# Gates of the second chunk scanned by themselves at the start of an mLSTM and Fourier-mix kernel

## The chip, the cores and the metric

The kernel runs on one core of one Trainium2 chip. The metric is the device time of one execution, in microseconds (us), as the median of several runs. Trace times are microseconds from the start of the profiled span. The engines are named as in the profile: PE is the matmul engine and PEld its weight loads, DVE the vector engine, ACT the engine of activations, POOL the general-purpose engine, and SP the one that issues the transfers.

## The reference, cut to what matters

The first block is an mLSTM cell over 4 batches of 8 heads, 768 tokens and a head dimension of 40; the second a Fourier mix with a two-layer MLP over the joined 320 features. All data are float32.

```python
for t in range(S):                                   # mLSTM, for every batch and head
    m_new = np.maximum(f_gate[t] + m, i_gate[t])     # running maximum
    f_stab, i_stab = np.exp(f_gate[t] + m - m_new), np.exp(i_gate[t] - m_new)
    m = m_new
    C = f_stab * C + i_stab * outer(v[t], k[t])
    n = f_stab * n + i_stab * k[t]
    y[t] = sigmoid(o_gate[t]) * (C @ q[t]) / np.maximum(np.abs(n @ q[t]), 1.0)
# x: y with the heads joined to 320 features
u = x + np.real(fft(fft(x, axis=1), axis=2))
out = u + relu(layernorm(u) @ w_ch1) @ w_ch2
```

## The kernel before, in words

**Chunks.** The 768 tokens are cut into 6 chunks (0 to 5) of 128. Within a chunk the recurrence becomes matrix products: scores of queries and keys (`mlstm_scores`, L458), times a matrix of exponentials W (`mlstm_exp`, L416, made on ACT; `mlstm_weigh`, L467, multiplies on DVE), times the values (`mlstm_from_chunk`, L482, PE). The state C carries what came earlier: `mlstm_from_state` (L473) reads it, `mlstm_to_state` (L489) makes a chunk's share on PE (the tile pc), and `mlstm_gather` (L503) brings on ACT the new state (L511) and the chunk's result (L524) out of PSUM and takes a tanh of the output gate (L529).

**Gates.** All this needs per-token numbers of the gates, which `gates` (L140) makes for all 4 batches and 8 heads at once: 32 partitions, one for each batch and head. `sums` (L190) is a running sum F of the forget gates within each chunk, a DVE scan. `maxima` (L194) subtracts F from the input gates (giving a), runs a second DVE scan for the running maximum M, and keeps nM and m_in, which are biases of later exponentials. `weights` (L238) makes `wk = exp(a + nM)` and `decay` (L242) makes `g = exp(m_in - M)`, one ACT instruction for each chunk. `columns` (L246) transposes a (j = 0) or wk (j = 1) on PE into a PSUM tile pt, so that tokens lie on partitions; a DVE copy brings that into colT. `spread_max` (L206) copies the maxima of four heads over all 128 partitions: a mask product in bf16 and then, for each head, a product of a one-hot column with M. That product is in float32 for the chunks 0 and 1. For the chunks 2 to 5 it is in bf16, with M cut by `parts` (L221), five POOL instructions, into three bf16 parts M3 whose sum is M. `spread_decay` (L230) does the like for g, into the tile pG.

Before the change chunk 0 goes through the gates alone, and the chunks 1 to 5 go through them together.

**Order.** The order of instructions on every engine is that in which the program issues them. After the lines written out in `gates`, calls are entered with `at(slot, phase, ...)` and issued by rising (slot, phase), where the phases EVAC, FILL, MAIN, FILL_PE are 0, 1, 2, 3. Chunk c of batch 0 begins at slot 3c. So in slot 4 ACT gets the gather of chunk 0 (FILL) and then the conversion of a block of MLP weights (FILL + 0.5, L351 and L352), and in slot 6 the exponentials of chunk 2. PE gets `decays` in slot 4 (tile pd), `spread_max` and `spread_decay` of chunk 2 at the end of slot 5, and in slot 6 `mlstm_from_state` and `mlstm_from_chunk` of chunk 1 and the scores of chunk 2.

**Buffers.** pt, the chunk results ph and the state shares pc take turns in two PSUM buffers (`ps_h`); the scores ps have two others (`ps_s`), which `mlstm_weigh` sets free.

Of the kernel before, what the change touches and what calls it, by code (L numbers as in the profile page):

```python
# [19 lines left out]
L = 128  # L20
NT = S // L
NP = H // 2
D1 = D + 1
BH = B * H
# [26 lines left out]
def kernel(  # L51
# [14 lines left out]
    nc = tc.nc  # L66
# [18 lines left out]
    def bank(name, shape, n=None):  # L85

        return ps_m.tile(shape, FP, name=name, tag=f"pm{next(turn) if n is None else n}")


    ident = const.tile([L, L], FP, name="ident")  # L90
# [6 lines left out]
    colT = const.tile([L, NT, 2, BH], FP, name="colT")  # L97
# [24 lines left out]
    def at(slot, phase, fn, *args):  # L122
        plan.setdefault((slot, phase), []).append((fn, args))
# [7 lines left out]
    EVAC, FILL, MAIN, FILL_PE = range(4)  # L131
# [8 lines left out]
    def gates(gp):  # L140
# [8 lines left out]
        M = gp.tile([L, NT, L], FP, name="M")  # L149
        wk = gp.tile([BH, NT, L], FP, name="wk")  # L150
        g = gp.tile([L, NT, L], FP, name="g")
        nM = gp.tile([BH, NT], FP, name="nM")
        M3 = gp.tile([3 * BH, NT, L], BF, name="M3")
        below = gp.tile([BH, NT, L], BF, name="below")
        sel = gp.tile([3 * BH, BH], BF, name="sel")
# [13 lines left out]
        nc.vector.memset(keep, 1.0)  # L169
        nc.vector.memset(keep[:, :, 0:1], 0.0)  # L170
        nc.vector.memset(shift, 0.0)
        nc.vector.memset(M[:, 0:2], 0.0)
        for t in C_bufs:
            nc.scalar.copy(out=t.rearrange("p (two n) t -> p two (n t)", two=2),
                           in_=rest.unsqueeze(1).to_broadcast([L, 2, 2 * L]))
# [11 lines left out]
        def flat(t, s):  # L187
            return t[0:BH, s].rearrange("p c t -> p (c t)")

        def sums(s):  # L190
            nc.vector.tensor_tensor_scan(out=flat(F, s), data0=flat(keep, s), data1=flat(f_sb, s), initial=0.0,
                                         op0=OP.mult, op1=OP.add)

        def maxima(s, initial):  # L194
            c0, c1 = s.start, s.stop
            nc.vector.tensor_tensor(out=a[:, s], in0=a[:, s], in1=F[:, s], op=OP.subtract)
            if c0 > 0:
                nc.vector.tensor_copy(out=shift[:, s, 0:1], in_=F[:, c0 - 1:c1 - 1, L - 1:L])
            nc.vector.tensor_tensor_scan(out=flat(M, s), data0=flat(shift, s), data1=flat(a, s), initial=initial,
                                         op0=OP.add, op1=OP.max)  # L200
            nc.vector.tensor_scalar(out=nM[:, s], in0=M[0:BH, s, L - 1], scalar1=-1.0, scalar2=None, op0=OP.mult)
            if c0 > 0:
                nc.vector.tensor_tensor(out=m_in[:, s], in0=M[0:BH, c0 - 1:c1 - 1, L - 1:L],
                                        in1=F[:, c0 - 1:c1 - 1, L - 1:L], op=OP.add)

        def spread_max(b, c, h0):  # L206

            k = chunks[b, c]
            if h0 == 0:
                k.W = wp.tile([L, H, L], FP, name="W", tag="W")  # L210
                k.M = []
            k.M.append(bank("pM", [L, NP, L]))
            nc.tensor.matmul(k.M[-1], ident_b, later_b.unsqueeze(1).to_broadcast([L, NP, L]), start=True, stop=False,
                             skip_group_check=True)
            for h in range(h0, h0 + NP):
                bh = b * H + h
                w, x = (ident[:, bh:bh + 1], M[:, c, :]) if c < 2 else (sel[:, bh:bh + 1], M3[:, c, :])
                nc.tensor.matmul(k.M[-1][:, h - h0, :], w.to_broadcast([w.shape[0], L]), x, start=False, stop=True,
                                 skip_group_check=True)

        def parts(s):  # L221

            m, rest_ = M[0:BH, s], shift[:, s]
            nc.gpsimd.tensor_copy(out=M3[0:BH, s], in_=m)
            nc.gpsimd.tensor_tensor(out=rest_, in0=m, in1=M3[0:BH, s], op=OP.subtract)
            nc.gpsimd.tensor_copy(out=below[:, s], in_=rest_)
            nc.gpsimd.tensor_copy(out=M3[BH:2 * BH, s], in_=rest_)
            nc.gpsimd.tensor_tensor(out=M3[2 * BH:, s], in0=rest_, in1=below[:, s], op=OP.subtract)

        def spread_decay(b, c):  # L230
            k = chunks[b, c]
            k.G = bank("pG", [L, NP, L])
            for h in range(H):
                r, bh = slice(h % 2 * 64, (h % 2 + 1) * 64), b * H + h
                nc.tensor.matmul(k.G[r, h // 2, :], ident[:, bh:bh + 1].to_broadcast([L, 64]), g[:, c, :],
                                 start=True, stop=True)

        def weights(s):  # L238
            for c in range(s.start, s.stop):
                nc.scalar.activation(out=wk[:, c], in_=a[:, c], func=AF.Exp, bias=nM[:, c:c + 1])  # L240

        def decay(s):  # L242
            for c in range(s.start, s.stop):
                nc.scalar.activation(out=g[0:BH, c], in_=M[0:BH, c], func=AF.Exp, scale=-1.0, bias=m_in[:, c])

        def columns(s, j):  # L246
            pt = ps_h.tile([L, NT, BH], FP, name="pt", tag="ph")
            for c in range(s.start, s.stop):
                nc.tensor.transpose(pt[:, c, :], (a, wk)[j][:, c, :], ident[0:BH, 0:BH])
            return pt  # L250

        first, others, last = slice(0, 1), slice(1, NT), slice(2, NT)
        sums(first)
        maxima(first, M_INIT)
        pt = columns(first, 0)
        nc.scalar.copy(out=colT[:, first, 0], in_=pt[:, first])
        weights(first)
        spread_max(0, 0, 0)
        pt = columns(first, 1)
        spread_max(0, 0, NP)  # L260
        mlstm_scores(0, 0)
        sums(others)
        mlstm_exp(0, 0, 0)
        nc.vector.tensor_copy(out=colT[:, first, 1], in_=pt[:, first])
        mlstm_exp(0, 0, NP)
        maxima(others, M[0:BH, 0, L - 1:L])
        pt = columns(others, 0)
        mlstm_load_o(0, 1)
        nc.vector.memset(g[:, 1:3], 0.0)
        nc.vector.tensor_copy(out=colT[:, others, 0], in_=pt[:, others])  # L270
        decay(slice(1, 2))
        weights(others)
        spread_max(0, 1, 0)
        spread_max(0, 1, NP)
        spread_decay(0, 1)
        pt = columns(others, 1)
        late = {"pt": pt}

        def clear(*tiles):
            for t in tiles:  # L280
                nc.gpsimd.memset(t, 0.0)

        def columns_late():
            nc.vector.tensor_copy(out=colT[:, others, 1], in_=late["pt"][:, others])

        def decay_late():
            decay(last)
            for hip in range(2):
                nc.sync.dma_start(out=G_d[1:NT, hip].rearrange("c p t -> p c t"), in_=g[hip:BH:2, 1:NT])

# [13 lines left out]
            nc.sync.dma_start(out=M_d.rearrange("c p t -> p c t"), in_=M[0:BH])  # L304

        at(12, FILL + 0.7, maxima_out)
        at(1, FILL + 0.2, parts, last)
        at(5, FILL_PE + 2.1, spread_decay, 0, 2)
        for c in range(2, NT):
            for h0 in (0, NP):  # L310
                at(3 * c - 1, FILL_PE + 2, spread_max, 0, c, h0)
        at(2, FILL + 0.5, columns_late)
        at(4, FILL - 0.4, decay_late)
        at(4, FILL + 0.5, decays)
        at(5, FILL - 0.5, decays_out)
# [95 lines left out]
    def mlstm_load_o(b, c):  # L411
        k = chunks[b, c]
        k.so = op_.tile([L, DM], FP, name="so", tag="so")
        nc.sync.dma_start(out=k.so, in_=o_gate[b, c])

    def mlstm_exp(b, c, h0):  # L416

        k = chunks[b, c]
        for h in range(h0, h0 + NP):
            M = k.M[h // NP][:, h % NP, :] if hasattr(k, "M") else k.W[:, h, :]  # L420
            nc.scalar.activation(out=k.W[:, h, :], in_=M, func=AF.Exp, scale=-1.0,  # L421
                                 bias=colT[:, c, 0, b * H + h:b * H + h + 1])
# [35 lines left out]
    def mlstm_scores(b, c):  # L458

        k = chunks[b, c]  # L460
        k.ps = [ps_s.tile([L, NP, L], FP, name=f"ps{hip}", tag="ps") for hip in range(2)]
        for p in range(NP):
            for hip in range(2):
                r = slice(hip * 64, hip * 64 + D)
                nc.tensor.matmul(k.ps[hip][:, p, :], k.qk[r, 1, p, :], k.qk[r, 0, p, :], start=True, stop=True)  # L465
# [599 lines left out]
    ctx.enter_context(tc.manual_schedule())  # L1065
    gates_pool = ExitStack()
    gates(gates_pool.enter_context(tc.tile_pool(name="gates", bufs=1)))


# [162 lines left out]
```

## Time and profile before

| | before |
|---|---|
| median of 3 runs (lowest to highest) | 422.28 us (421.28 to 422.81) |
| span of the profiled execution | 419.2 us |
| PE busy | 408.1 us, 97% |
| DVE busy | 288.8 us, 69% |
| ACT busy | 189.5 us, 45% |
| POOL busy | 112.9 us, 27% |
| PE busy between 4 and 20 us | 15.43 of 16 us |
| ACT busy between 12 and 20 us | 7.71 of 8 us |

The busy shares are means over a span with different stages; the change lies in the first 25 us. There PE and ACT are both nearly full, and DVE and POOL are busy for about three quarters and half of the time. The timeline lists the instructions of each engine in order, neighbours of one kind merged: start, duration, engine, line, operation, result and inputs, shapes and count.

### The profile page before, as it was taken

What the parts mean: (1) busy time and instruction counts of PE and PEld (TensorE: products, weight loads), DVE (VectorE), ACT (ScalarE), POOL (GpSimd) and SP (SyncE); (2) the same over time, 40 slices, a digit from 0 to 9 for tenths busy, and PEclk for the clock granted to TensorE, in tenths of its full rate; (3) what the DMA queues carried; (4) which work ended last, traced back from release to release, by engine and by line L of the source; (5) the groups of instructions that cost most, each with busy time, mean ns of one, the idle gap of its engine ahead of it and who ended that gap; (6) DMA issues with size and microseconds to landing.
All of it is one profiled execution on the core that took longest, in us unless ns stands there. A gap on an engine that the chain in (4) does not pass through costs nothing.

```text
span 419.2 us, 8001 instructions
## 1 busy us (share of the span) xinstructions
PE 408.1 (97%) x2966; PEld 302.4 (72%) x2966; DVE 288.8 (69%) x682; ACT 189.5 (45%) x493; POOL 112.9 (27%) x194
## 2 busy tenths in 40 slices
PE   8999999999999999999999999999999999999997
PEld 6877555566567778776549998976559988455996
DVE  8789895777895638777765569788663786335652
ACT  6986376686561222654455413744451113355000
POOL 5554201468431520442231430351220000020000
PEclk9999999999999999999999999999999999999999
DMA  7899297567765254276100554310000000000010
GB/s 230 288 250 318 71 278 257 185 162 219 236 189 164 59 155 139 64 210 197 50 0 2 156 149 131 100 42 1 0 2 0 33 31 34 0 2 0 16 48 31
DMA packets 20549, 47.14 MB, mean 112 GB/s; under 512 B 2784, under 2 KB 9312, under 8 KB 20384
## 3 DMA queue, kind: packets, MB, share of 16 engines
q1 hardware_dynamic: 20512, 46.65, 36.7%
q8 instruction: 23, 0.38, 0.4%
q14 instruction: 14, 0.11, 0.1%
HBM read 42.52 MB, written 4.11 MB: 111 GB/s over the span
## 4 chain that ended last, share of the span: by engine, by line
PE 82%; DVE 7%; DMA 4%; issue 3%; ACT 2%; POOL 1%; ACTq 0%; DVEq 0%; POOLq 0%; SPq 0%
PE po L999 18%; PE pm L897 17%; PE po L943 8%; PE pm L902 5%; PE ps L465 5%; PE ph L486 4%; PE pu L729 4%; PE ph L479 3%; PE pm L837 3%; DMA raw<-in_w 3%; PE px L535 2%; PE put L772 2%; PE pz L698 2%; DMA kvt<-in_kv 1%; PE pz L686 1%
## 5 line engine op out<-in xcount | busy, mean ns | idle before, releaser
L949 DVE SCALAR_TENSOR_TENSOR x<-po,rstd,x 128x160 f32<-128x160 f32 (+1 forms) x69 | 27.0, 395 | 40.2 <-PE po L999 34.1
L906 DVE TENSOR_TENSOR h<-h,pm 128x384 f32<-128x384 f32 x60 | 30.5, 550 | 30.5 <-ACT h L919 20.9
L421 ACT ACTIVATE W<-W,colT 128x128 f32<-128x128 f32 x144 | 45.0, 395 | 0.0
L443 POOL TENSOR_SCALAR_AFFINE_SELECT W<-W 128x1024 f32<-128x1024 f32 x18 | 21.6, 1198 | 81.0 <-ACT W L421 59.1
L943 PE MATMUL po<-w_sb,h 128*128 128x320 f32 x120 | 34.4, 435 | 0.0
L897 PE MATMUL pm<-uT,w_sb 128*128 128x384 f32 x90 | 32.8, 492 | 0.2 <-DVE uT L885 0.2
L471 DVE TENSOR_TENSOR W<-ps,W 128x512 f32<-128x512 f32 x48 | 30.7, 680 | 2.6 <-POOL W L443 2.4
L837 PE MATMUL pm<-uT,w_sb 128*128 128x384 f32 x80 | 29.6, 499 | 0.7 <-DVE x L749 0.5
L777 ACT COPY uT<-put 128x384 f32<-128x384 f32 x24 | 11.2, 478 | 40.2 <-PE put L772 40.2
L943 PEld LDWEIGHTS po<-w_sb,h 128*128 128x128 f32 x120 | 22.2, 190 | 9.5 <-issue 0.8
L999 PE MATMUL po<-T,S 128*128 128x160 f32 x180 | 27.9, 302 | 0.6 <-DVE x L949 0.6
L465 PE MATMUL ps<-qk 40*128 40x128 f32 x384 | 27.8, 284 | 0.0
L999 PEld LDWEIGHTS po<-T,S 128*128 128x128 f32 x180 | 25.5, 190 | 2.2 <-DVE x L949 1.0
L792 POOL TENSOR_TENSOR t<-rstd 128x6 f32<-128x6 f32 x12 | 2.9, 244 | 89.2 <-DVE v L790 88.6
L999 PE MATMUL po<-w_sb,h 128*128 128x160 f32 x180 | 26.4, 301 | 0.0
L465 PEld LDWEIGHTS ps<-qk 40*128 40x128 f32 x384 | 23.4, 187 | 4.1 <-issue 0.7
L999 PEld LDWEIGHTS po<-w_sb,h 128*128 128x128 f32 x180 | 25.1, 190 | 1.3 <-DVE x L949 0.3
L486 PE MATMUL ph<-W,kvt 128*41 128x128 f32 x384 | 25.8, 277 | 0.0
L431 POOL TENSOR_TENSOR qg<-qk,Gb 128x512 f32<-128x512 f32 x18 | 25.2, 1402 | 0.1
L524 ACT COPY h<-ph 41x512 f32<-41x512 f32 (+1 forms) x16 | 9.3, 583 | 34.9 <-PE ph L486 34.8
L479 PEld LDWEIGHTS ph<-qg,C 128*128 128x128 f32 x160 | 20.0, 191 | 6.3 <-issue 2.5
L897 PEld LDWEIGHTS pm<-uT,w_sb 128*128 128x128 f32 x90 | 16.2, 190 | 10.8 <-DVE h L906 1.5
(207 smaller groups left out, 864.6 us busy)
## 6 DMA issues: line engine op xcount, KB each, us to landing
W<-M_d SPq DMA_DIRECT2D x18, 512.0 KB
kvt<-in_kv SPq DMA_DIRECT2D x24, 324.0 KB
qk<-in_qkT SPq DMA_DIRECT2D x48, 160.0 KB
raw<-in_w SPq DMA_DIRECT2D x10, 640.0 KB
Gb<-G_d SPq DMA_DIRECT2D x36, 128.0 KB
so<-in_o SPq DMA_DIRECT2D x24, 160.0 KB
out<-x SPq DMA_DIRECT2D x24, 160.0 KB
ds_sb<-in_dft_s SPq DMA_DIRECT2D x1, 1155.0 KB
```

The lines of the kernel that those rows point to most:

```text
L421: nc.scalar.activation(out=k.W[:, h, :], in_=M, func=AF.Exp, scale=-1.0, bias=colT[:, c, 0, b * H + h:b * H + h + 1])
L431: nc.gpsimd.tensor_tensor(out=k.qg, in0=k.qk[:, 0], in1=k.Gb, op=OP.mult)
L465: nc.tensor.matmul(k.ps[hip][:, p, :], k.qk[r, 1, p, :], k.qk[r, 0, p, :], start=True, stop=True)
L471: nc.vector.tensor_tensor(out=Wv, in0=k.ps[hip], in1=Wv, op=OP.mult)
L479: nc.tensor.matmul(k.ph[:, p, :], k.C[:, p, :], k.qg[:, p, :], start=(p == 0), stop=False, skip_group_check=True)
L486: nc.tensor.matmul(k.ph[hip * 64:hip * 64 + D1, p, :], k.v1[:, 2 * p + hip, :], k.W[:, 2 * p + hip, :], start=(c == 0 and p == 0), stop=Tr ...
L837: nc.tensor.matmul(k.pm[i], w1_sb[:, ch, f0:f0 + L], u[2 * ch], start=(ch == 0), stop=False)
L897: nc.tensor.matmul(bank, w, u, start=start, stop=True, skip_group_check=True)
L906: nc.vector.tensor_tensor(out=h, in0=h, in1=bank, op=OP.add)
L943: nc.tensor.matmul(k.po, hidden(gr, f)[:, i * L:(i + 1) * L], w2_sb[:, f, :], start=(f == 0), stop=(f == NFF - 1))
L949: nc.vector.scalar_tensor_tensor(out=u, in0=po, scalar=k.rstd[:, c:c + 1], in1=u, op0=OP.mult, op1=OP.add)
L999: nc.tensor.matmul(po, a[:, f], w[:, f], start=start and f == 0, stop=f == half - 1, skip_group_check=True)
```

## The change

The gates of chunk 1 now go through the scans by themselves, directly after those of chunk 0, and those of the chunks 2 to 5 after them. Chunk 1's maxima are also cut into three bf16 parts, so that its `spread_max` uses the bf16 form. The purpose is to have what chunk 1 needs earlier, and to keep the other chunks' exponentials (`weights(others)`) from standing in front of those of chunk 1 on ACT: they go into the plan at slot 5, with their transpositions (`columns_last`) late in slot 5 and the copy into colT early in slot 6.

```diff
-        nc.vector.memset(M[:, 0:2], 0.0)
+        nc.vector.memset(M[:, 0:1], 0.0)
...
-                w, x = (ident[:, bh:bh + 1], M[:, c, :]) if c < 2 else (sel[:, bh:bh + 1], M3[:, c, :])
+                w, x = (ident[:, bh:bh + 1], M[:, c, :]) if c == 0 else (sel[:, bh:bh + 1], M3[:, c, :])
...
-        first, others, last = slice(0, 1), slice(1, NT), slice(2, NT)
+        first, second, others = slice(0, 1), slice(1, 2), slice(2, NT)
+        def columns_out(s, j, pt):
+            nc.vector.tensor_copy(out=colT[:, s, j], in_=pt[:, s])
...
         spread_max(0, 0, 0)
         pt = columns(first, 1)
+        sums(second)
+        maxima(second, M[0:BH, 0, L - 1:L])
+        parts(second)
+        columns_out(first, 1, pt)
+        pt = columns(second, 0)
         spread_max(0, 0, NP)
         mlstm_scores(0, 0)
+        mlstm_exp(0, 0, 0)
+        mlstm_exp(0, 0, NP)
+        mlstm_load_o(0, 1)
+        columns_out(second, 0, pt)
+        nc.vector.memset(g[:, 1:3], 0.0)
         sums(others)
-        mlstm_exp(0, 0, 0)
-        nc.vector.tensor_copy(out=colT[:, first, 1], in_=pt[:, first])
-        mlstm_exp(0, 0, NP)
-        maxima(others, M[0:BH, 0, L - 1:L])
-        pt = columns(others, 0)
-        mlstm_load_o(0, 1)
-        nc.vector.memset(g[:, 1:3], 0.0)
-        nc.vector.tensor_copy(out=colT[:, others, 0], in_=pt[:, others])
-        decay(slice(1, 2))
-        weights(others)
+        maxima(others, M[0:BH, 1, L - 1:L])
+        decay(second)
+        weights(second)
         spread_max(0, 1, 0)
         spread_max(0, 1, NP)
         spread_decay(0, 1)
-        pt = columns(others, 1)
-        late = {"pt": pt}
+        late = {1: columns(second, 1), 0: columns(others, 0)}
...
         def columns_late():
-            nc.vector.tensor_copy(out=colT[:, others, 1], in_=late["pt"][:, others])
+            columns_out(second, 1, late[1])
+            columns_out(others, 0, late[0])
+        def columns_last():
+            late[2] = columns(others, 1)
         def decay_late():
-            decay(last)
+            decay(others)
...
-        at(1, FILL + 0.2, parts, last)
+        at(1, FILL + 0.2, parts, others)
+        at(5, FILL + 0.3, weights, others)
+        at(5, FILL_PE + 1.8, columns_last)
+        at(6, FILL - 0.2, lambda: columns_out(others, 1, late[2]))
         at(5, FILL_PE + 2.1, spread_decay, 0, 2)
```

## The prediction

> **What bounds the kernel now.** I read the page first: busy shares, then the chain that ended last.
>
> ```profile
> PE 408.1 (97%) x2966; PEld 302.4 (72%) x2966; DVE 288.8 (69%) x682; ACT 189.5 (45%) x493; POOL 112.9 (27%) x194
> PE 82%; DVE 7%; DMA 4%; issue 3%; ACT 2%; POOL 1%; ACTq 0%; DVEq 0%; POOLq 0%; SPq 0%
> ```
>
> PE is busy for 97% of the span and carries 82% of the chain. So the end follows PE's queue: what delays PE early delays the end, unless a later idle stretch takes it up. After 24 us the gaps between PE's matmuls that are over 0.12 us add up to about 6 us, in pieces of at most 0.82 us.
>
> Next the chain in order of time, in the stage that the change touches.
>
> ```profile
> 16.14 0.44 PE pd L297 x2
> 16.58 0.32 PE pM L213
> 16.90 0.23 PE pM L218 x4
> 17.13 0.22 PE pM L213
> 17.35 0.23 PE pM L218 x4
> 17.57 1.02 PE pG L235 x16
> 18.60 1.09 PE ph L479 x8
> 19.68 1.09 PE ps L465 x16
> 20.78 1.00 PE ph L486 x16
> ```
>
> Columns are start, duration, engine, tile, line, count. The reader is to see that from pd on PE runs straight through: maxima and decay of chunk 2, then chunk 1's read of the state, chunk 2's scores, chunk 1's product with its values. Nothing here waits for ACT.
>
> (The chain also holds a transfer of kvt, 5.96 us from 36.87. I don't take it as a bound: no compute engine in the list of waits up to 50 us waits for a transfer, and PE works through most of that stretch.)
>
> Last the timeline of ACT from 10 to 20 us, with PE's and DVE's rows that matter.
>
> ```profile
> 10.62 1.26 DVE L471 TENSOR_TENSOR W<-ps,W 128x512 f32<-128x512 f32 x2
> 10.85 1.55 ACT L240 ACTIVATE wk<-a,nM 32x128 f32<-32x128 f32 x5
> 12.31 2.09 ACT L421 ACTIVATE W<-pM,colT 128x128 f32<-128x128 f32 x8
> 13.25 1.16 PE L465 MATMUL ps<-qk 40*128 40x128 f32 x16
> 14.31 1.26 ACT L244 ACTIVATE g<-M,m_in 32x128 f32<-32x128 f32 x4
> 15.24 0.48 PE L496 MATMUL pc<-vw,kvt 128*40 128x41 f32 x16
> 15.77 0.60 ACT L511 COPY C<-pc 40x164 f32<-40x164 f32 x2 [0.19 <-PE pc L496]
> 16.39 1.17 ACT L524 COPY h<-ph 41x512 f32<-41x512 f32 x2
> 16.51 0.39 PE L213 MATMUL pM<-later_b,ident_b 128*128 128x512 bf16 x1
> 17.59 0.47 ACT L529 ACTIVATE so<-so 128x320 f32<-128x320 f32 x1
> 17.96 0.82 ACT L351 ACTIVATE e<-e,ebias 128x640 uint32<-128x640 uint32 x1
> 18.68 0.72 ACT L352 ACTIVATE m<-m 128x640 f32<-128x640 uint32 x1
> 19.43 2.18 ACT L421 ACTIVATE W<-pM,colT 128x128 f32<-128x128 f32 x8
> ```
>
> ACT is full. From the end of pc (15.24 + 0.48 = 15.72) it needs until 19.43 for the gather of chunk 0 and the weight conversion. PE in that time is already at chunk 2's spread (16.51) and beyond.
>
> **What the Trainium skill says.** "TensorE: Matmul & The Clock Gate", section on the array's architectural detail, has ACT and DVE as strict FIFO, and PE as able to pull only weight loads ahead. The trace agrees: each engine's rows stand in program order. The same page, under what actually happens in the clock gate, halves PE's clock after an idle window of about 3.4 us and frees it after about as long a busy one. The trace fits its warm-up half: eight float32 matmuls of L218 take 1.48 us from 4.75 and 1.05 us from 6.57. "SBUF — State Buffer", who interferes with whom, has an exclusive lock between POOL and DVE instructions that use DVE's second port. The trace agrees: a DVE copy of 5 elements a partition (L198) takes 0.69 us and ends at 7.98, as POOL's vw ends at 7.95.
>
> **The change part by part.**
>
> *Bf16 spread for chunk 1.* In the chain the float32 form is 0.89 us for eight matmuls, and the bf16 form 0.23 us for four. Two halves save 2 x (0.89 - 0.23) = 1.32 us of PE. The M3 parts cost POOL five instructions on 128 elements instead of 512. At 512 the rows are 0.60 and 1.15 us; a quarter of the length lies between a quarter and all of that, and I take about 0.3 each with gaps, 1.7 us, from 5.6 (after chunk 1's scan) to 7.3. PE needs M3 only after the scores of chunk 0 at about 8.8, so that work hides it. The wait of 0.45 us for DVE's scan, ahead of the weights of L218 at 9.61, goes.
>
> *Fewer transpositions early.* PE has 6 instead of 10 ahead of chunk 1's scores (after chunk 0's own), about 0.06 us each: 0.24 us saved.
>
> So PE could begin chunk 1's scores early. Chunk 0's scores end at 8.8; two bf16 halves take 0.45 each (9.7); pG 1.02 (10.7), with its g from ACT at about 9.2, since ACT's exponentials of chunk 0 end at 8.81; five transpositions 0.3: 11.0, against 13.25.
>
> *The second scan on DVE.* It takes much of that back. Chunk 1's gates fit into the idle time from 4.4 to 6.45. Then come two colT copies and the memset of g (to 7.2), and the scans of 4 chunks: 0.35 us is the F scan of 128 elements and 1.47 that of 640, 2.19 ns an element, so 1.19 us for 512; likewise 1.25 for M (0.41 and 1.54). Subtraction 0.65, shift copy 0.1, nM and m_in 0.6. Sum: 7.2 + 1.19 + 0.65 + 0.1 + 1.25 + 0.6 = about 11.0. Only then does chunk 0's weighing (L471, 1.26 us) follow, ending at 12.3, or 13.0 if POOL's vw (0.73 us where nothing disturbs it) gets in front. It frees the two score buffers, so chunk 1's scores start at 12.35 to 13.05 instead of 13.25. From their start to the end of pc it is 15.72 - 13.25 = 2.47 us: pc ends at 14.8 to 15.5. Kept gain: 0.2 to 0.9 us.
>
> *The other chunks' exponentials.* Taking four of them out of the front lets ACT finish chunk 1's exponentials at about 11.8 and g at 13.1. But there ACT has to wait for pc, so this is worth nothing beyond the shift above.
>
> *The new wait.* This decides. `weights(others)` stands in slot 5, on ACT behind slot 4's gather and weight conversion. `columns_last` transposes its results on PE ahead of chunk 2's `spread_max`. Queued behind it on PE are that, pG, chunk 1's `mlstm_from_state`, chunk 2's scores and chunk 1's `mlstm_from_chunk`: all the rows of the second fence after pd. From the end of pc ACT needs 0.05 to start, 3.66 us to the end of the conversion (15.77 to 19.43), then four wk, 0.29 apart and the last 0.39 long: 0.87 + 0.39 = 1.26. The last wk is there 4.97 us after pc, the last transposition and the first mask product about 0.1 later: 5.1. Before, the mask product began 16.51 - 15.72 = 0.79 after pc. So PE loses 5.1 - 0.79 = 4.3 us; only pd (0.44) lies in its wait. ACT's exponentials of chunk 2, DVE's colT copy, and behind that on DVE qg and the join of the weights wait with it.
>
> *Sum.* 4.3 - 0.9 = +3.4 to 4.3 - 0.2 = +4.1 us at chunk 2's spread; middle 3.7. From there every wait is of the same kind as before, so I carry it to the end: 422.28 + 3.7 = 426.0. Transfers don't take it up: their engines rest from 45 to 50 us, and SP issues when buffers come free, which moves along. The memset of M and the moved loads cost nothing beside this.
>
> **The rivals.**
>
> *A: as above*, 425 to 427, 426.0.
>
> *B: the wait also drops PE's clock.* PE would rest from about 16 to 20 us, 3.6 to 4.4 us. Against the skill's window of 3.4 us, whose position isn't tied to the kernel, that may just suffice. Then some 3.4 us or more at half speed cost about 2.5 more: 428.5. For it: the slow matmuls at the start. Against it: no rest that long in the trace after the start, so nothing here shows the drop, and a whole window must fall into the rest.
>
> *C: the early gain is kept.* If DVE's order costs less than I think, PE keeps all of the 2.25 us (13.25 - 11.0), and the loss is 4.3 - 2.25 = 2.05: 424.3; with some slack later about 423.8. For it: DVE's numbers are chained from short rows. Against it: the score buffers hang on one DVE row that has four chunks' scans in front of it.
>
> *D: faster.* If the transpositions in fact don't hold PE (wk done in time by an ACT that has run ahead), what remains is the saving of 1.32 + 0.24 and perhaps the wait of 0.15 between matmuls: 422.28 - 1.7 = 420.6. Against it: the gather waits for pc and stands ahead of wk on a FIFO.
>
> **How the numbers follow.** A 0.62, B 0.15, C 0.13, D 0.10. Half a per cent is 2.1 us: slower is above 424.4. A and B are slower, and a quarter of C: 0.80. The rest of C and a little of D are the same: 0.11. Faster 0.09. The range goes from 423.2 (part of C) to 428.8 (most of B).
>
> **What would show it.** Right: in the changed kernel PE waits about 4 us at L249 for ACT's L240, whose four rows stand behind L352; the first mask product of chunk 2 lies near 20.2 instead of 16.51; chunk 1's spread shows four matmuls for each half; PE waits for DVE's L471 before L465, near 12. Rival B would show the L218 and L235 rows after that wait at about twice their time. It is wrong if PE's wait at L249 is under 2 us, or if chunk 1's product with its values starts before 22 us (20.78 before).

## The result, and the profile after

| | before | after |
|---|---|---|
| median (lowest to highest) | 421.87 us (421.28 to 422.81), 4 runs | 428.50 us (427.86 to 429.19), 4 runs |
| ratio | | 1.0155, 95% interval 1.0127 to 1.0184 |
| span of the profiled execution | 419.2 us | 427.5 us |
| mean granted clock of PE in it | 0.999 | 0.984 |

The change makes the kernel slower by 1.6%, 6.6 us. First the page of the changed kernel: busy shares, PE's clock in 40 slices of the span (tenths of full speed), and the chain by engine.

```profile
PE 412.9 (97%) x2958; PEld 305.4 (71%) x2958; DVE 289.0 (68%) x690; ACT 189.3 (44%) x493; POOL 116.8 (27%) x199
PEclk9669999999999999999999999999999999999999
PE 83%; DVE 10%; ACT 3%; issue 2%; POOL 0%; ACTq 0%; DVEq 0%; POOLq 0%
```

The shares stay as they were. What is new is the 66 in the clock's second and third slices, between about 11 and 32 us. Next the chain in order of time, from the second half of chunk 0's product with its values.

```profile
16.23 0.57 PE pc L510 x16
16.83 0.29 ACT C L525
17.13 0.30 ACT C L525
17.44 0.58 ACT h L538
18.03 0.58 ACT h L538
18.64 0.47 ACT so L543
19.11 0.72 ACT e L365
19.82 0.62 ACT m L366
20.45 0.30 ACT wk L240
20.79 1.19 PE pt L249 x4
21.98 0.54 PE pM L213
22.52 0.43 PE pM L218 x4
22.95 0.43 PE pM L213
23.37 0.43 PE pM L218 x4
23.80 1.91 PE pG L235 x16
25.70 2.01 PE ph L493 x8
27.71 1.20 PE ps L479 x16
28.91 1.00 PE ph L500 x16
```

Before, this stretch was PE alone. Now the chain leaves PE at the end of pc, runs through ACT's whole queue (gather, tanh, weight conversion, first wk), and comes back at the transpositions. After that, pG takes 1.91 us instead of 1.02 and the read of the state 2.01 instead of 1.09: half speed. The timeline of PE's rows around both waits:

```profile
12.62 1.75 PE L479 MATMUL ps<-qk 40*128 40x128 f32 x16 [0.64 <-DVE W L485]
14.30 1.93 PE L500 MATMUL ph<-W,kvt 128*41 128x128 f32 x16
16.71 0.71 PE L308 MATMUL pd<-dec,spread_sb 32*128 32x80 f32 x2
20.79 1.19 PE L249 MATMUL pt<-ident,wk 32*128 32x32 f32 x4 [3.37 <-ACT wk L240]
28.84 1.07 PE L500 MATMUL ph<-W,kvt 128*41 128x128 f32 x16
```

The long wait is 3.37 us. Chunk 1's product with its values starts at 28.84, where it was 20.71 in the trace before: 8.1 us later, nearly the whole 8.3 us by which the two spans differ. What comes after 29 us adds only about 0.2 us in all. (The spans differ by more than the medians, since the profiled executions took 429.19 and 420.94 us.) That L500 takes 1.93 us at 14.30 already and 1.07 at 28.84 shows that the clock was halved before the long wait began. The windows view, with PE busy, its clock, and the transfers:

```profile
10.84:14.25 3.41, 2.66 (x35) 2.11 (x31) 3.38 (x10) 2.55 (x10) 2.76 (x3) 1.00 1.04 308
14.25:17.66 3.41, 3.17 (x36) 2.69 (x34) 1.01 (x5) 0.81 (x3) 3.07 (x4) 0.50 0.83 296
17.66:21.08 3.42, 0.29 (x1) 0.17 (x1) 1.23 (x3) 3.38 (x8) 1.07 (x3) 0.50 0.69 225
21.08:24.49 3.41, 3.41 (x22) 2.36 (x23) 0.29 (x1) 2.04 (x8) 1.03 (x4) 0.50 0.52 161
24.49:27.90 3.41, 3.41 (x22) 2.86 (x20) 2.09 (x3) 0.67 (x3) 0.00 (x0) 0.50 0.02 6
27.90:31.30 3.40, 3.40 (x62) 2.79 (x62) 2.99 (x6) 0.71 (x3) 0.38 (x1) 1.00 0.66 187
```

After the duration come the busy times of PE, PEld, DVE, ACT and POOL, and PE's clock stands third from the end. It is half from 14.25 to 27.90 us: 13.65 us, four times 3.41. The mean clocks of the four runs tell that this varies. At 0.983 and 0.984 they took 428.91 and 429.19 us, at 0.991 and 0.992 they took 427.86 and 428.08. By estimate from these means, the latter two ran at half speed for about 7 us.

### The profile page after: what moved, and what is told of

Same layout as the page of the kernel before. It is cut to its first block, busy times and chain, and to the rows that moved or that the text cites. A ratio compares the mean times of both kernels' runs of the same rounds, so it can differ in the third digit from the quotient of the medians.

```text
span 427.5 us, 7999 instructions
## 1 busy us (share of the span) xinstructions
PE 412.9 (97%) x2958; PEld 305.4 (71%) x2958; DVE 289.0 (68%) x690; ACT 189.3 (44%) x493; POOL 116.8 (27%) x199
## 4 chain that ended last, share of the span: by engine, by line
PE 83%; DVE 10%; ACT 3%; issue 2%; POOL 0%; ACTq 0%; DVEq 0%; POOLq 0%
PE po L1013 18%; PE pm L911 17%; PE po L957 8%; PE pm L916 5%; PE ph L500 5%; PE ps L479 5%; PE pm L851 5%; PE ph L493 4%; PE pu L743 3%; PE put L786 2%; PE px L549 2%; PE pz L712 2%; DVE W L485 1%; PE pm L855 1%; PE pz L700 1%
## 5 line engine op out<-in xcount | busy, mean ns | idle before, releaser
L500 PE MATMUL ph<-W,kvt 128*41 128x128 f32 x384 | 26.7, 282 | 0.0
L493 PE MATMUL ph<-qg,C 128*128 128x128 f32 x160 | 22.7, 286 | 1.6 <-POOL eo L632 0.8
```

The source lines that it names most:

```text
L493: nc.tensor.matmul(k.ph[:, p, :], k.C[:, p, :], k.qg[:, p, :], start=(p == 0), stop=False, skip_group_check=True)
L500: nc.tensor.matmul(k.ph[hip * 64:hip * 64 + D1, p, :], k.v1[:, 2 * p + hip, :], k.W[:, 2 * p + hip, :], start=(c == 0 and p == 0), stop=Tr ...
```

## The experiments

My theory was that two costs add up, the wait of PE for the late exponentials and the halved clock that rest on PE brings. The main rival was that the order of the scans on DVE at the front costs the time, and that the wait at L249 (the transpositions of `columns_last`) only shows it. In each diff, - is the changed kernel unless another is named. A median of the kernel before, taken beside each group of runs, was 421.92 to 422.09.

**The late exponentials alone.** The kernel before, with `last` for the chunks 2 to 5, its scans untouched:

```diff
-        weights(others)
+        weights(slice(1, 2))
...
-        pt = columns(others, 1)
-        late = {"pt": pt}
+        late = {"pt": columns(slice(1, 2), 1)}
...
+        at(5, FILL + 0.3, weights, last)
+        at(5, FILL_PE + 1.8, columns_last)
+        at(6, FILL - 0.2, columns_last_out)
```

> The kernel before with nothing of the change but the late place of the four exponentials, their transpositions and their copy; the scans stay together and chunk 1's maxima in float32. Theory: the same wait at L249, 5.1 us after pc instead of 0.79 for the mask product: 426 to 429, by whether the clock drops. Rival of the DVE order: 422 to 422.5.

Measured: 428.29 us (427.30 to 429.35), ratio 1.0156 (1.0124 to 1.0187). This is the whole loss of the change, without one of its scans or bf16 products. Its timeline shows the same queue on ACT and the same wait:

```profile
15.35 0.48 PE L504 MATMUL pc<-vw,kvt 128*40 128x41 f32 x16
18.78 0.72 ACT L360 ACTIVATE m<-m 128x640 f32<-128x640 uint32 x1
19.40 1.26 ACT L240 ACTIVATE wk<-a,nM 32x128 f32<-32x128 f32 x4
19.84 1.19 PE L249 MATMUL pt<-ident,wk 32*128 32x32 f32 x4 [2.90 <-ACT wk L240]
22.78 1.98 PE L235 MATMUL pG<-g,ident 128*64 128x128 f32 x16
```

The mean clock is below full in all four runs (0.991 to 0.996). In the profile it falls towards the end of the long wait, with PE's busy time first in each row and its clock third from the end:

```profile
16.08:19.49 3.41, 0.44 (x2) 0.29 (x2) 1.80 (x5) 3.35 (x8) 1.07 (x3) 1.00 0.67 226
19.49:22.90 3.41, 3.06 (x16) 1.90 (x18) 0.29 (x1) 2.04 (x9) 1.03 (x4) 0.50 0.59 181
```

**The exponentials early.** Only their place is altered, to ahead of chunk 0's gather, where ACT rested 3.43 us for pc:

```diff
-        at(5, FILL + 0.3, weights, others)
+        at(4, FILL - 0.3, weights, others)
```

> Theory (the place of the late exponentials costs the time: PE waits at the transpositions of columns_last for ACT, and its clock drops besides): with the four exponentials ahead of chunk 0's gather, where ACT rests, the wait of 3.4 us at L249 goes. What stays is a wait for the PSUM buffer, which the gather frees 1.85 us after pc. Chunk 2's first mask product at 17.0 to 17.6, time 422.5 to 424. Rival (the order of the scans on DVE at the front costs the time, and the wait at L249 only shows it): 427 or more.

Measured: 421.69 us over 20 runs (419.82 to 427.92), ratio 0.9996 (0.9972 to 1.002). One moved call undoes the loss. The rest of the wait is shorter than I expected:

```profile
14.94 0.60 ACT L525 COPY C<-pc 40x164 f32<-40x164 f32 x2 [0.54 <-PE pc L510]
15.60 0.43 PE L249 MATMUL pt<-ident,wk 32*128 32x32 f32 x4 [0.25 <-ACT C L525]
```

The transpositions take over the PSUM buffer of pc, not that of ph, and so start as soon as L525 has copied the state out, 0.7 us after pc and not 1.85. The first mask product of chunk 2 is at 15.96, and the time lies below the range that I gave.

The clock is still part of it: seven of these 20 runs had a mean clock of 0.987 to 0.996 and took 422.72 to 427.92 us, while the other 13 had a median of 421.18. Of the 31 runs of the kernel before beside them, two were below full clock (424.98 and 426.88), and the other 29 had a median of 422.02.

**And the transpositions behind the spread.**

```diff
-        at(5, FILL + 0.3, weights, others)
+        at(4, FILL - 0.3, weights, others)
-        at(5, FILL_PE + 1.8, columns_last)
+        at(5, FILL_PE + 2.2, columns_last)
```

> Theory: with the transpositions also behind chunk 2's spread and pG, PE waits for nothing of ACT there. POOL's last part of the maxima (it ended at 16.72 in the changed kernel) is then what the first mask products wait for, so about 16.5 to 16.8 for them, as before, and 421 to 422.5 in all. Rival of the DVE order: 426 or more.

Measured: 421.48 us over 12 runs (420.40 to 428.17), ratio 0.9994 (0.9969 to 1.002), the first mask product at 15.66, and behind it a wait of 0.20 us for POOL's last part, which ended at 16.20. The time is as expected, but no better than that of the version above. Two of the 12 runs had a mean clock below full (0.980 and 0.992).

**The transpositions behind the spread, the exponentials still late.** Only the second line of the diff above.

> The changed kernel with nothing altered but columns_last behind chunk 2's spread and pG; the exponentials stay late on ACT. Theory: the wait moves behind 2.1 us of PE work and shrinks by that, to about 2 us, too short for a drop of the clock in most runs: 423.5 to 424.5. Rival (the wait on ACT sets chunk 1's product whatever stands ahead of it): 425.5 or more.

Measured: 423.55 us, ratio 1.0051 (1.0026 to 1.0076).

```profile
16.50 1.09 PE L235 MATMUL pG<-g,ident 128*64 128x128 f32 x16
18.79 1.12 PE L249 MATMUL pt<-ident,wk 32*128 32x32 f32 x4 [1.19 <-ACT wk L240]
22.02 1.07 PE L500 MATMUL ph<-W,kvt 128*41 128x128 f32 x16
```

Chunk 2's spread and pG now fill part of the wait, of which 1.19 us are left in one piece, with some tenths between the transpositions. So the loss shrinks when PE has other work to do while ACT works. Three of the ten runs had a mean clock of 0.992, and these were the three longest (424.53 to 427.18).

**PE kept busy in the waits.** Products of zeros, which nothing reads, into a free bank:

```diff
+        def keep_busy(n, b):
+            pw = bank("pi", [L, 2 * L], b)
+            for i in range(n):
+                nc.tensor.matmul(pw, rest[:, 0:L], rest, start=True, stop=True, skip_group_check=True)
...
+        at(3, FILL_PE + 1.9, keep_busy, 2, 1)
+        at(5, FILL_PE + 1.7, keep_busy, 8, 0)
```

> The changed kernel with products of zeros on PE in its two waits (2 ahead of chunk 1's scores, 8 ahead of columns_last), which nothing reads. Theory (wait and clock are two costs): the clock stays full, and the wait alone remains, 3.4 to 4.1 us over before: 425.3 to 426.3. Rival (the clock adds nothing, all is the wait): no change against the changed kernel, 427.9 to 429. Rival (nearly all is the clock): 422.5 to 423.5.

Measured: 425.91 us (425.16 to 427.41), ratio 1.0103 (1.0069 to 1.0138), clock full in all runs.

```profile
14.37 0.47 PE L517 MATMUL pc<-vw,kvt 128*40 128x41 f32 x16
15.15 3.72 PE L297 MATMUL pi<-rest 128*128 128x256 f32 x16
18.87 1.12 PE L249 MATMUL pt<-ident,wk 32*128 32x32 f32 x4
20.91 1.09 PE L235 MATMUL pG<-g,ident 128*64 128x128 f32 x16
24.11 1.07 PE L507 MATMUL ph<-W,kvt 128*41 128x128 f32 x16
```

More work on PE, and a faster kernel: the added 3.72 us stand in the wait, pG is back at 1.09 us, and chunk 1's product comes at 24.11, 3.4 us later than before the change instead of 8.1. This separates the two costs: 425.91 - 422.07 = 3.8 us for the wait, 428.50 - 425.91 = 2.6 us for the clock (the runs of 428.50 were of an earlier group, with 421.87 for the kernel before). Their intervals against the kernel before overlap a little, but the runs themselves don't (427.41 at most here, 427.86 at least there).

**Busy in the second wait only.** The first of the two `keep_busy` calls is left out.

> The changed kernel with products of zeros only in the second wait (ahead of columns_last), none ahead of chunk 1's scores. If the rest of about a microsecond around chunk 1's scores alone drops the clock in some runs, as the profile of the changed kernel reads: a drop of one window from about 14 us, 425.5 to 427.5. If only the long wait drops it: as with both filled, 425.2 to 426.5, and the clock full.

Measured: 425.52 us (425.01 to 426.75), ratio 1.0092 (1.0065 to 1.0119). Three runs had the full clock. The profiled one, 426.75 us, had not, and it shows where:

```profile
10.27:13.68 3.41, 2.44 (x32) 1.96 (x33) 3.38 (x8) 2.99 (x11) 2.20 (x3) 1.00 1.02 306
13.68:17.10 3.42, 3.42 (x44) 3.06 (x40) 1.37 (x4) 0.00 (x0) 3.21 (x4) 0.50 0.87 316
```

A window with about a microsecond of rest around chunk 1's scores (3.41 - 2.44) was followed by 3.4 us at half speed, and the run took about 1.4 us longer than the other three (mean 425.35). The same program kept the full clock in those three, so such a rest doesn't always bring the fall; with both waits filled no run had one.

**Where the early gain went.** Four versions start from the second repair (exponentials early, transpositions behind the spread). First chunk 1's spread in float32 again:

```diff
-        nc.vector.memset(M[:, 0:1], 0.0)
+        nc.vector.memset(M[:, 0:2], 0.0)
...
-                w, x = (ident[:, bh:bh + 1], M[:, c, :]) if c == 0 else (sel[:, bh:bh + 1], M3[:, c, :])
+                w, x = (ident[:, bh:bh + 1], M[:, c, :]) if c < 2 else (sel[:, bh:bh + 1], M3[:, c, :])
...
-        parts(second)
```

> The version with the four exponentials early and the transpositions behind the spread, with chunk 1's maxima spread in float32 again (and no parts of chunk 1 on POOL). If the 1.32 us that the bf16 products save on PE reach the end: 422.6 to 423.2. If PE's waits (for POOL's last part of chunk 1, 0.67 us, for DVE's weighing, and for POOL's last part of the other chunks, 0.20 us) already give them back: no change, 421 to 422.

Measured: 421.72 us, ratio 0.9987 (0.9973 to 1.0002), against 421.48 and 0.9994 with bf16. The 1.32 us of PE that bf16 saves don't reach the end. In the bf16 version PE waits for POOL instead. POOL's cast L226 takes 1.10 us beside DVE's scan there, against 0.28 us in the changed kernel, where no scan ran beside it:

```profile
7.33 1.17 DVE L191 TENSOR_TENSOR_SCAN F<-keep,f_sb 32x512 f32<-32x512 f32 x1
7.49 1.10 POOL L226 CAST below<-shift 32x128 bf16<-32x128 f32 x1
9.92 0.38 PE L218 MATMUL pM<-M,sel 96*128 96x128 bf16 x4 [0.67 <-POOL M L228]
```

Then the weighing of chunk 0 ahead of the later scans, with POOL's parts in two pieces:

```diff
         sums(others)
+        mlstm_weigh(0, 0)
...
-        at(1, FILL + 0.2, parts, others)
+        at(1, FILL + 0.2, parts, slice(2, 3))
+        at(3, FILL + 0.3, parts, slice(3, NT))
-        at(4, FILL - 0.3, weights, others)
+        at(4, FILL + 0.1, weights, others)
...
-            at(s + 1 if end else s + 2, FILL - 0.4 if end else FILL, mlstm_weigh, b, c)
+            if (b, c) > (0, 0):
+                at(s + 1 if end else s + 2, FILL - 0.4 if end else FILL, mlstm_weigh, b, c)
```

> The same version with chunk 0's weighing on DVE ahead of the scans of the chunks 2 to 5, and POOL's parts of chunk 2 ahead of those of 3 to 5. Theory (the early gain is given back at the score buffers and at POOL's parts): PE starts chunk 1's scores about 0.6 to 1 us earlier, and the time falls to 420.3 to 421.2. Rival (the gather on ACT, now later behind decays and exponentials that wait for the later scan, takes it back): 421.2 to 422.5.

Measured: 422.09 us, ratio 1.0005 (0.9991 to 1.002). A miss. Chunk 1's scores did come at 11.16 instead of 12.22, but the parts of three chunks on POOL held up the state's decay, for which PE waited 0.90 us at 22.12, and the gain was gone. So I spread those parts over the chunks:

```diff
-        at(3, FILL + 0.3, parts, slice(3, NT))
+        for c in range(3, NT):
+            at(3 * c - 3, FILL + 0.2, parts, slice(c, c + 1))
```

> The version with chunk 0's weighing ahead of the later scans, with POOL's parts of the chunks 3, 4 and 5 one by one, each two slots ahead of its use. There POOL's parts of three chunks at once held up the state's decay, for which PE waited 0.90 us at 22.12. Theory (this was what took the gain back): the wait goes, chunk 2's product with its values starts about 0.9 us earlier, 420.6 to 421.3. Rival (PE gets no more, since other waits follow): 421.7 to 422.4.

> The same with chunk 1's maxima spread in float32 and no parts of it on POOL. The bf16 products save PE up to 1.32 us, but now nothing on DVE holds up chunk 1's scores, so that this should show: 1 to 1.3 us above the version with bf16. If POOL's parts cost as much as the products save: equal within 0.5 us.

Measured: 422.58 us (421.17 to 429.35), ratio 1.0005 (0.9992 to 1.0018), and with float32 423.32 us, 1.0033 (1.002 to 1.0046). The first is another miss: the wait moved to chunk 3's spread, 0.94 us for POOL's L228, at 23.59 and 23.66 in the profiles of the two. In the second pair the float32 form is slower by 0.7 us, between the two outcomes that I had named; the intervals of both don't overlap. But not all of this is the spread: in every run of the float32 version 2.1 to 2.2 us of the time lie outside the span from the first to the last instruction, in the bf16 version 1.7 to 1.8. That is over half of the difference, and no run here explains it. None of these versions beats the kernel before by more than its uncertainty.

## Why the prediction was right or wrong

It forecast slower, 426.0 us in a range of 423.2 to 428.8; the result is 428.50. By its steps:

- **The new wait** was right in kind, place and size. It had the first mask product of chunk 2 at 5.1 us after pc; in the changed kernel pc ends at 16.78 and the product starts at 21.91, 5.13 later. The experiments show that it is the cause: alone it costs the whole loss, and taking it away ends the loss.
- **The sum of 3.4 to 4.1 us** was right for the wait without the clock: 425.91 and 425.52 with PE kept busy, with pc ending at 14.84 in the profile with both waits filled (forecast 14.8 to 15.5). In the changed kernel's own profile, at half speed from 14.25, pc ends at 16.78.
- **The clock** was the term that the likeliest case left out. It stood as rival B, with 2.5 us and a chance of 0.15. B's 428.5 is what was measured, its sign is in the trace (pG at 1.91 us instead of 1.02), and the clock's share came out as 2.6 us. What failed is the condition that the prediction took from the Trainium skill ("TensorE: Matmul & The Clock Gate", what's actually happening), that a whole window of about 3.4 us must fall into the rest; the low chance rested on it in part. The traces here differ from it: with the late exponentials alone the clock fell after a window in which PE was busy for 0.44 us, in the changed kernel after one with 2.66 us. That second fall came at 14.25, before the long wait, after 0.75 us of rest around chunk 1's scores, which I had sized as a loss of gain only. The fall was not in one run but in all four, and also in all four of the version with the late exponentials alone. That 2.5 us came so close is partly luck: it stood for "some 3.4 us or more" at half speed, and the runs had about 7 to 13.65 us.
- **The early part.** Chunk 0's weighing was forecast to end between 12.3 and 13.0 and ended at 13.16; chunk 1's scores waited for it as forecast. The copy between DVE's two scans, put at 0.1 us, took 0.69 and ended at 9.97, as POOL's vw (the values times wk) ended at 9.95. POOL's parts of chunk 1 were taken as hidden, done at 7.3. They ended at 8.81, as the last instruction took 1.48 us beside DVE's scan. In this profile PE's slow start hid even that, as chunk 0's scores ended at 9.53 only. In profiles of other versions, where they ended earlier, PE waited 0.39 to 0.67 us for the parts.
- **Rival C** (2.25 us of early gain kept) fell: even with the wait removed, bf16 and the separate scan end level with the kernel before by their medians. The runs at full clock alone, 421.18 against 422.02, are 0.8 us ahead, within the 0.2 to 0.9 us that the likeliest case kept.
- **Rival D** (faster) fell: the gather stood ahead of wk as its counter-argument said.

What stays open: where the small gains of the repaired versions go. Some may go to the clock. The two bf16 versions with chunk 0's weighing in its old place had it below full in nine of 32 runs, and the float32 version and the two bf16 versions with the weighing moved ahead in none of 46 (0.998 or more); the float32 version with the weighing moved ahead had it below in two of 22 (0.995 and 0.996). That points to the rest around chunk 1's scores, but these groups ran on different chips, and no run isolates it. At chunk 2's product with its values (26.33 us before) the profiles of the three with chunk 0's weighing in its old place are 0.1 to 0.9 us ahead, and the medians hardly show it. In one of them (exponentials early) a product at 71.45 waits 1.39 us, by the profile for a transfer, and a lead of 0.4 us turns into a lag of 1.1. Whether that is the rule wasn't tested.

## What to carry to other kernels

Moving work to a later place in one engine's queue is not free when another engine's in-order queue meets its result: look at what stands ahead of it on its own queue, and what stands behind the reader. Adding up what stands ahead on the producer's queue gave the time at which the reader's next work starts to within 0.1 us here. Where the waiting engine is PE, add the clock: rests of about one and three microseconds together cost a further 2.6 us here, and products of zeros in the waits gave that back.

## What the runs showed of the hardware

- The clock fell and rose in steps of 3.41 us: 13.65 us at half speed in the changed kernel (four), 6.8 in the late exponentials alone (two), 3.4 with only the second wait filled (one).
- It fell after windows in which PE was busy for 0.44 us (the late exponentials alone), but also for 2.66 and for 2.44 of 3.41 us; in these two no rest was longer than 0.86 us in one piece. Yet with only the transpositions behind the spread a window with less work than these two passed without a fall:

```profile
15.68:19.09 3.41, 2.11 (x27) 1.53 (x26) 1.01 (x2) 3.37 (x8) 1.81 (x5) 1.00 0.79 273
```

So PE's busy time in the profile doesn't settle whether the clock falls, and I have no rule for it.
- PE's slow start varies between executions: the same eight matmuls of L218 for chunk 0 took 1.91 us from 4.76 in the changed kernel's profile and 1.05 from 4.57 in that of the float32 version, whose code for PE is the same up to there.
- A short POOL instruction and a DVE scan side by side got in each other's way. With the transpositions behind the spread and the exponentials early, POOL's cast L226 of 32x128, begun 0.16 us after a scan, took 1.10 us, against 0.28 us where no scan ran. In the same profile the subtraction L228, begun 0.01 us after the second scan, kept to 0.42 us, and it was the scan that took longer: 1.51 us, against 1.27 in the changed kernel.
